# State attention and a Mish feed-forward on one core: a new order of every engine's instructions, contiguous halves of the first input, and a shorter last sum

## The chip, the cores and the metric

The kernel runs on one core of a Trainium2 chip. The metric is the device time of one execution in microseconds; the profile is of one execution, and its span runs from the first instruction to the last.

## The reference

For each of 8 batches and 8 heads, x (512 rows of 64) and a state (32 rows of 64) attend to each other in both directions. Both results go, heads side by side, as rows of 512 into a feed-forward layer of width 2048 with the Mish function.

```python
B, H, S, Ns, D = (8, 8, 512, 32, 64)          # n_tokens 4608 = 8 * (512 + 32), d_model 512, d_ff 2048
scores = scale * np.matmul(x, state.transpose(0, 1, 3, 2))
a = softmax(scores)
xread = np.matmul(a, state)
scores2 = scale * np.matmul(state, x.transpose(0, 1, 3, 2))
a2 = softmax(scores2)
sread = np.matmul(a2, x)
attn = np.concatenate([xread, sread], axis=2)  # then (B * S, H * D)
h = attn @ w_in
g = h * np.tanh(log1p(exp(h)))                 # Mish
return g @ w_out
```

## The kernel before

Since xread = a @ state, the product xread @ w_in is computed as a @ (state @ w_in): for each batch the kernel forms sw = state @ w_in (128 rows, one for each head and state row, by 2048), and multiplies the turned probabilities with it. The feed-forward width is cut into 8 slots of 256 columns.

Each large product is three matmuls of fp32r operands, 128x128 against 128x256: high by high, high by low and low by high parts. ACT writes a rounded copy (the high part) and DVE subtracts it from the original (the low part).

Batches 0 and 1 run while the weights still arrive and are split ("wide": `p`, `ma`/`mb`, `gh`, `gl`, `g`, `o` in the order strings). From batch 2 (`FIRST`) on, the work is in units of half a batch, two units for a batch, and at the end one unit of all batches' state rows. A unit has 8 periods, one for each slot, and the steps of period n are:

- `P_n` (gemm1): 12 matmuls into one of two PSUM banks (`ps_h`), 24 in the last unit. `M_n` (mish, ACT) reads that bank, so the bank is free for the next but one `P`.
- `S_n` (sums, DVE, 3 instructions), `H_n` (high, ACT), `L_n` (low, DVE): they make the seven operands of the second product, which is done with seven block products in place of eight (Strassen's scheme).
- `U_n` and `V_n` (gemm2): 12 and 9 matmuls that accumulate into four PSUM banks over the 8 periods; `U` is banks 0 and 1, `V` banks 2 and 3.
- `C` (combine): at the end of a unit one copy and 8 additions turn the four banks into the output, which is stored.

Beside this the next batch's attention runs, with letters a, b, c for a batch and the next ones:

- `SC`: 32 small matmuls (64x32 weights) give the scores; `sc tu to le x1 ts no ba ph pl` are its softmax, turns and split on ACT and DVE.
- `t2 x2 s2 TU BU RE ro`: the other direction; `TU` and `BU` go through DRAM, `RE` is 64 small matmuls (128x32 weights).
- `SX_0` and `SX_4`, each two calls of `SW` (32 small matmuls each): sw for slots 0 to 3 and 4 to 7. `xh` and `xl` split them on ACT and DVE. `SX_j` takes slots j and j+1 through the two `ps_h` banks and slots j+2 and j+3 through the two misc banks.
- `in_e` (stream): SP loads slot e of w_in (512 KB) back from `w_dram`. Slots 0 and 4 share the buffer wi6, 1 and 5 share wi7; 2, 3 and 6, 7 share the two halves of the buffer `x`. So `in_4` must wait until `SX_0` has read slot 0. `LX`, `LN` and `LS` load x, its other layout and the state, in the same buffers.

The order on each engine is written out by hand. `InOrder` ties every instruction of TensorE, DVE, ACT and SP to the one before it on that engine, so PE, for example, runs exactly in the order of the text. Batches 0 and 1 and unit 0 follow the string `OPENING`; every later period n follows the loop, which issues gemm1(n+2), high(n+1), low(n+1), mish(n+2), U(n), V(n), sums(n+2), with the other steps put in by tables (`STEADY`, `LAST`, `END`) keyed by the period.

In the opening PE also runs `fill` and `warm_up` matmuls (identity by identity), which compute nothing that is used.

The last output (state rows) is 8 transfers, four for each half of the tile `o`, all issued by SP.

Of the kernel before, what the change touches and what calls it, by code (L numbers as in the profile page):

```python
# [63 lines left out]
def state_attention_mish_kernel(ctx, tc, xT, xn, st, wiw, wow, out):  # L64
# [705 lines left out]
    run(OPENING, a=0, b=1, c=2, d=3)  # L770

    for n, (u, s) in enumerate(periods):
        if n < SLOTS:
            continue
        b, h = u
        now = SLOTS * h + s
        table = END if b == "s" else LAST if b == B - 1 else STEADY
        extra = {k: [v] for k, v in table.get(now, {}).items()}

        def beside(place):  # L780
            who = {} if b == "s" else dict(a=b, b=b + 1, c=b + 2)
            for text in extra.get(place, ()):
                run(text, **who)

        one, two = n + 1 < len(periods), n + 2 < len(periods)
        if two:
            gemm1(n + 2)
        beside("a0")
        if one:
            high(n + 1)  # L790
        beside("v0")
        if one:
            low(n + 1)
        beside("a1")
        if two:
            mish(n + 2)
        gemm2(n, 0)
        beside("pe")
        gemm2(n, 1)
        beside("pe2")  # L800
        beside("v1")
        if two:
            sums(n + 2)
        beside("a2")
        if s == SLOTS - 1:
            combine(u)
        beside("v2")
# [3 lines left out]
    lb tab lx_0 sca_0 sma_0 sma_1 lx_1 li_0 fill_1 tur_0 sca_1 top_0 sma_2 li_1 sma_3 li_2 lev_0 tur_1 Lo_0  # L811
    top_1 ev_0 tot_0 gua_0 rec_0 ci_0 hi_0 lev_1 ev_1 hi_1 warm nor_0 bac_0 ji_0 a.SW_0 pih_0 tot_1 gua_1 pil_0
    rec_1 a.wh_0 a.wl_0 hi_2 nor_1 di_2 pq_0 Lo_1 bac_1 ci_1 ji_1 ho_0 a.SW_1 js_0 li_5 li_3 pih_1 co_0 pil_1
    fill_2 fill_2 ji_2 a.wh_1 mh_0 a.wl_1 jo_0 pq_1 mh_1 a.SW_2 ho_1 a.wh_2 wo_0 gi_1 ci_5 lo_0 gj_1 gi_0 a.wl_2
    p_1 hi_3 ci_3 gj_0 ma_1 do_1 mb_1 ji_3 gh_1 g_3 g_2 jo_1 Lo_6 g_1 g_0 gl_1 a.SW_3 a.wh_3 a.wl_3 p_2 b.LX
    Lo_2 ma_2 mb_2 wo_1 lo_1 Lo_4 ho_2 p_3 hi_5 Lo_3 co_3 li_4 hi_4 g_10 do_2 gh_2 jo_2 g_13 g_12 wo_2 lo_2 gl_2
    ci_4 ji_4 ho_4 g_11 ho_3 jo_3 wo_3 ji_5 g_20 Lo_5 ho_5 li_6 g_23 a.SW_4 a.wh_4 co_5 a.wl_4 lo_3 mb_3 g_22
    g_21 ma_3 a.SW_5 p_4 js_2 co_4 gh_3 gl_3 jo_4 b.LS hi_6 ci_6 a.t2 a.wh_5 ma_4 mb_4 gh_4 a.wl_5 g_32 li_7
    wo_4 g_30 g_33 ji_6 p_5 Lo_7 gl_4 lo_4 a.x2_1 a.SW_6 a.wh_6 a.wl_6 js_5 g_31 g_41 g_42 a.x2_0 jo_5 co_6 ho_6
    g_43 ma_5 mb_5 ci_7 a.TU wo_5 lo_5 js_3 a.s2 g_40 js_6 hi_7 b.SC p_6 b.sc_1 gh_5 gl_5 b.sc_0 ji_7 g_53  # L820
    a.SW_7 mb_6 ma_6 jo_6 wo_6 b.tu b.to a.wh_7 a.wl_7 gh_6 g_50 b.le g_51 ho_7 b.x1 lo_6 b.SW_0 gl_6 p_7 js_4
    g_52 g_61 ma_7 b.wh_0 mb_7 b.ts b.no js_1 b.ba g_60 co_7 a.BU b.ph_0 a.LN b.ph_1 b.wl_0 g_62 g_63 b.pl_0
    a.RE b.LN b.pl_1 p_8 gh_7 gl_7 a.ro js_7 jo_7 wo_7 ma_8 mb_8 b.SW_2 p_9 lo_7 g_70 g_71 g_72 b.wh_2 b.wl_2
    gh_8 gl_8 mb_9 g_73 o_0 ma_9 p_10 gh_9 gl_9 mb_10 b.t2 o_1 b.SW_6 ma_10 b.wh_6 p_11 g_83 g_93 gh_10 b.wl_6
    o_2 o_3 g_81 g_91 b.SW_4 gl_10 b.x2_1 g_80 b.x2_0 c.LX ma_11 b.TU qs_0 b.wh_4 b.wl_4 g_101 qs_1 c.LS c.SC
    g_82 kh_0 kl_0 mb_11 qh_0 gh_11 gl_11 g_92 p_12 c.sc_0 ql_0 d.LS g_90 in_1 c.sc_1 in_0 c.SW_0 mb_12 qs_6
    g_102 c.wh_0 c.tu g_103 c.to kh_1 ma_12 g_113 g_100 c.le g_110 c.x1 g_112 g_111 in_5 c.t2 gh_12 gl_12 c.x2_0
    b.s2 c.wl_0 qh_1 c.ts p_13 g_121 ql_1 ma_13 c.no kl_1 mb_13 gh_13 qs_7 g_122 c.x2_1 qh_7 p_14 b.BU b.RE in_4
    gl_13 g_123 qh_6 c.ba in_2 ql_6 c.ph_0 ql_7 c.pl_0 g_133 ma_14 g_131 g_132 g_120 mb_14 b.ro qs_4 qh_4 ql_4
    in_3 c.SW_2 gh_14 g_130 c.wh_2 gl_14 c.wl_2 p_15 g_140 qs_5 ma_15 P_0 qh_5 c.SW_4 g_141 qs_3 g_142 ql_5  # L830
    mb_15 gh_15 kh_3 gl_15 qh_3 g_150 g_143 c.TU M_0 g_151 S_0 in_6 c.wh_4 in_7 kl_3 H_0 o_4 ql_3 P_1 o_5 g_152
    g_153 c.wl_4 M_1 L_0 S_1 o_6 c.ph_1 H_1 L_1 o_7 P_2 U_0 V_0 P_3 M_2 d.LX kh_7 S_2 qs_2 V_1 P_4 H_2 kh_2 kl_2
    qh_2 L_2 kh_4 kl_4 ql_2 kl_7 M_3 c.pl_1 M_4 U_1 S_3 c.SW_6 c.BU c.wh_6 kh_5 c.wl_6 c.s2 U_2 P_5 H_3 V_2 L_3
    c.LN S_4 M_5 kl_5 S_5 H_4 L_4 d.SC P_6 V_3 V_4 kh_6 kl_6 U_3 in_0 d.sc_0 M_6 S_6 d.sc_1 c.RE H_5 U_4 d.tu
    c.ro H_6 d.to P_7 L_5 U_5 L_6 V_5 M_7 S_7 H_7 d.le P_8 M_8 L_7 V_6 U_6 S_8 H_8 d.t2 L_8 P_9 in_2 U_7 M_9 S_9
    V_7 in_3 C_0 in_1
# [3 lines left out]
STEADY = {  # L840
    2: dict(pe="a.RE", pe2="b.SC", v1="a.ro", a2="b.sc_0 b.sc_1", v2="in_0 in_1 in_2 in_3"),
    3: dict(v0="b.tu"),
    4: dict(v0="b.to"),
    5: dict(v0="b.le"),
    6: dict(v0="b.t2"),
    8: dict(a2="b.x1 b.x2_0 b.x2_1"),
    9: dict(v0="b.ts b.s2", v2="b.no"),
    10: dict(v2="b.ba"),
    11: dict(pe="b.SX_0", a2="b.xh_0", v2="b.xl_0 in_4 in_5 in_6 in_7"),
    12: dict(a2="b.ph_0 b.ph_1", v2="b.pl_0 b.pl_1"),  # L850
    13: dict(v2="b.TU b.BU"),
    14: dict(pe="b.SX_4", a2="b.xh_4", v2="b.xl_4 b.LN c.LX c.LS"),
}
LAST = {
    0: dict(v2="in_0 in_1"),
    2: dict(pe="a.RE", v1="a.ro", v2="in_2 in_3"),
    7: dict(pe="ST", a2="sh", v2="sl"),
    12: dict(a2="WH_0", v2="WL_0 in_4"),
    13: dict(a2="WH_1", v2="WL_1 in_5"),
    14: dict(a2="WH_2", v2="WL_2"),  # L860
    15: dict(a2="WH_3", v2="WL_3 in_6 in_7"),
}
END = {
    0: dict(a2="WH_4", v2="WL_4"),
    1: dict(a2="WH_5", v2="WL_5"),
    2: dict(a2="WH_6", v2="WL_6"),
    3: dict(a2="WH_7", v2="WL_7"),
}
# [28 lines left out]
```

## Time and profile before

| | us |
|---|---|
| median of 3 runs (lowest to highest) | 634.57 (631.49 to 635.59) |
| the profiled execution | 632.25 |
| its span | 630.5 |
| PE busy in the span | 609.2 |
| DVE busy | 478.3 |
| ACT busy | 339.3 |

The profiled execution is 1.75 us longer than its span. The granted TensorE clock has a mean of 0.994 over the span. Busy times of different engines overlap and don't add up; for PE a busy stretch may still run at different rates, so the distance from one matmul's start to the next is read beside it.

### The profile page before, as it was taken

The numbers are of one execution on the slowest core, as the hardware profiler recorded it, in microseconds if no ns is written. First come the engines' busy times: TensorE is split into PE (matmuls) and PEld (weight loads), VectorE is DVE, ScalarE is ACT, GpSimd is POOL, SyncE is SP. The second block draws the span as 40 slices with busy tenths as digits, with TensorE's granted clock in tenths as the row PEclk, the third lists the DMA queues.
The fourth block names the chain that finished last, engine by engine and source line by source line (L and its number), as shares of the span: only waits on it lengthen the run. The fifth ranks groups of instructions, "written<-read, shape, count | busy, mean of one in ns | idle before, by whom it ended". The sixth has DMA issues, their size and how long they took to land.

```text
span 630.5 us, 15205 instructions
## 1 busy us (share of the span) xinstructions
PE 609.2 (97%) x6548; PEld 582.9 (92%) x6548; DVE 478.3 (76%) x874; ACT 339.3 (54%) x497; POOL 0.7 (0%) x6
## 2 busy tenths in 40 slices
PE   4899999899999999999999999999999999999995
PEld 3798899899999999999999999999999999999995
DVE  4786896589788888588868797679858886577753
ACT  4988763456355564347634754456534663445541
POOL 0000000000000000000000000000000000000000
PEclk9899999999999999999999999999999999999998
DMA  8976443642175234601563047403551165101201
GB/s 334 411 306 269 126 150 111 171 165 68 20 217 199 68 131 145 200 40 45 158 210 134 35 137 233 142 35 114 164 191 45 40 169 202 61 35 68 102 1 33
DMA packets 57267, 86.43 MB, mean 137 GB/s; under 512 B 35825, under 2 KB 38897, under 8 KB 54001
## 3 DMA queue, kind: packets, MB, share of 16 engines
q1 hardware_dynamic: 57056, 85.34, 40.2%
q8 instruction: 51, 0.84, 0.5%
q14 instruction: 16, 0.12, 0.1%
q10 hardware_dynamic: 144, 0.13, 0.1%
...
## 4 chain that ended last, share of the span: by engine, by line
PE 90%; ACT 4%; DVE 2%; DMA 2%; issue 1%; SPq 1%; DVEq 0%; ACTq 0%
...
## 5 line engine op out<-in xcount | busy, mean ns | idle before, releaser
L56 ACT CAST Sh<-G 128x896 fp32r<-128x896 f32 x104 | 98.2, 944 | 134.7 <-DVE G L56 48.7
L56 PE MATMUL ph_u<-aT,sw 128*128 128x256 f32 x1152 | 150.2, 280 | 0.0
L56 DVE TENSOR_TENSOR Sl<-G,Sh 128x896 fp32r<-128x896 f32 x104 | 112.9, 1086 | 44.7 <-ACT Sh L56 44.2
L56 PEld LDWEIGHTS ph_u<-aT,sw 128*128 128x128 f32 x1152 | 141.0, 189 | 2.1 <-issue 2.1
L56 DVE TENSOR_TENSOR G<-G 128x128 f32<-128x128 f32 (+1 forms) x312 | 104.7, 335 | 22.0 <-ACT G L56 14.2
L56 PE MATMUL acc<-wo,gh 128*128 128x256 f32 x512 | 90.1, 280 | 0.0
L56 ACT ACTIVATE G<-ph_u 128x512 f32<-128x512 f32 x104 | 62.2, 599 | 49.3 <-PE ph_u L56 45.9
L56 PEld LDWEIGHTS acc<-wo,gh 128*128 128x128 f32 x512 | 77.4, 188 | 3.4 <-issue 3.3
L56 PE MATMUL acc<-wo,gl 128*128 128x256 f32 x256 | 71.1, 278 | 0.0
L56 PEld LDWEIGHTS ph<-aT,sw 128*128 128x128 f32 x384 | 47.0, 193 | 8.4 <-ACT turned L56 5.0
L56 PE MATMUL ph<-aT,sw 128*128 128x256 f32 x384 | 50.3, 287 | 4.0 <-ACT turned L56 2.5
L56 ACT CAST sw<-swp 128x512 fp32r<-128x512 f32 (+1 forms) x72 | 34.3, 549 | 29.4 <-PE swp L56 29.4
L56 PEld LDWEIGHTS acc<-wo,gl 128*128 128x128 f32 x256 | 48.4, 189 | 0.0
L56 DVE TENSOR_TENSOR sw<-swp,sw 128x512 fp32r<-128x512 f32 (+1 forms) x72 | 41.0, 623 | 9.5 <-ACT sw L56 9.5
...
L56 PE MATMUL swp<-wi,bd 64*32 64x256 f32 x1024 | 33.8, 381 | 0.6 <-DVE wi L56 0.5
L56 ACT ACTIVATE turned<-ph 128x512 f32<-128x512 f32 (+1 forms) x34 | 18.5, 574 | 20.8 <-PE ph L56 16.1
L56 DVE STREAM_TRANSPOSE e<-sc 128x512 f32<-128x512 f32 x30 | 19.5, 688 | 9.5 <-ACT sc L56 9.3
...
L56 DVE CAST gh<-turned 128x1024 fp32r<-128x1024 f32 (+1 forms) x17 | 11.2, 660 | 16.3 <-ACT turned L56 9.2
L56 PE MATMUL ph_u<-srT,whl 128*128 128x256 f32 x192 | 23.1, 276 | 0.0
L56 PEld LDWEIGHTS ph_u<-srT,whl 128*128 128x128 f32 x192 | 22.4, 188 | 0.0
...
## 6 DMA issues: line engine op xcount, KB each, us to landing
...
out_dram<-o SPq DMA_DIRECT2D x32, 256.0 KB, 3.2
...
```

The lines of the kernel that those rows point to most:

```text
L56: made = method(*args, **kwargs)
```

## The change

The parts, and what each does:

- Batch 0's x comes as two arrays of halves, `x0T[h]`, contiguous in DRAM (4 KB for each partition), where before each half was cut out of a larger row in pieces of 512 bytes. Half 1 is loaded first.
- `fill` and `warm_up` multiply a zero tile, and there are more of them; `nudge` is one more small matmul of zeros.
- `sw_four` runs the two slots of the misc banks first, those of the `ps_h` banks second, in the product and in both splits.
- The block product b22 goes from bank 2 to bank 3, beside q4. So the last two additions of `combine` (256 wide, from two banks) become one of 512.
- The state rows are stored by 2 transfers in place of 8, one issued by SP and one by ACT.
- `OPENING` is rewritten. The loop and its tables are replaced by two strings, `STEADY` (run once for each of batches 2 to 6) and `CLOSING` (batch 7 and the state rows). In `STEADY` a unit's `V` comes ahead of its `U` at the start, and the small blocks `SX_0`, `SX_4`, `SC` and `RE` stand at other places.

```diff
     def load_x0(h):
-        sp.dma_start(t, xT[0][:, :, :, cols(h)])
+        sp.dma_start(t, x0T[h])
...
         def fill(self, n, pt):
             for _ in range(n):
-                pe.matmul(pt[:, :P], ident, ident, start=True, stop=True)
+                pe.matmul(pt[:, :P], zero, zero, start=True, stop=True)
...
     PRODUCTS = [(0, 0, 0, "b11"), (0, 1, 2, "b21"), (1, 0, 5, "q6"), (1, 1, 3, "q7"), (2, 0, 4, "q5"),
-                (2, 1, 6, "b22"), (3, 0, 1, "q4")]
+                (3, 0, 6, "b22"), (3, 1, 1, "q4")]
...
-        dve.tensor_add(c12, c12, m3)
-        dve.tensor_add(c21, c21, m4)
+        inner = o.rearrange("p r e -> p (r e)")[:, HALF:3 * HALF]
+        dve.tensor_add(inner, inner, acc(u, 3))
...
-                for b4 in range(4):
-                    r0 = (4 * (1 - r) + b4) * T + S
-                    sp.dma_start(out[r0:r0 + NS, :], o[cols(b4, NS), r])
+                to = out.rearrange("(b t) e -> b t e", t=T)[4 * (1 - r):4 * (2 - r), S:]
+                (act if r else sp).dma_start(to, o[:, r])
...
-        for i, bank in ((j, first_bank), (j + 2, misc)):
+        for i, bank in ((j + 2, misc), (j, first_bank)):
             sw_step(b, i, what, 2, bank)
...
+    def nudge(i):
+        pt = misc(f"nudge_{i}")
+        pe.matmul(pt[:NS, :D], zero[:D, :NS], zero[:D, :D], start=True, stop=True)
...
+    run(OPENING, 0, "abcd")
+    for b in range(FIRST, B - 1):
+        run(STEADY, b, "abc")
+    run(CLOSING, B - 1, "a")
...
 OPENING = """
+    lb tab lx_1 fill_1 fill_1 fill_1 fill_1 fill_1 fill_1 fill_1 fill_1 fill_1 fill_1 sca_1 sma_2 sma_3 lx_0
+    sca_0 sma_0 sma_1 tur_1 tur_0 top_1 fill_1 fill_1 fill_1 top_0 a.t2 les_1 li_0 lev_0 nudge_0 ci_0 warm ex_1
+    fill_1 fill_2 tot_1 gua_1 hi_0 ji_0 li_1 rec_1 a.SW_0 hi_1 nor_1 ev_0 bac_1 tot_0 ci_1 li_2 gua_0 hi_2 Lo_0
+    ji_1 fill_2 fill_2 a.wh_0 pih_1 fill_2 fill_2 rec_0 nor_0 bac_0 Lo_1 ho_0 pil_1 a.wl_0 b.LS fill_2 pih_0
+    fill_2 a.SW_1 pil_0 pq_1 co_0 a.wh_1 fill_2 ho_1 mh_1 li_5 di_2 pq_0 mh_0 gk_1 a.wl_1 b.LX gk_0 ji_2 ci_5
...
+STEADY = """
+    H_9 P_10 c.LS L_9 V_8 P_11 U_8 V_9 M_10 S_10 b.x1 b.x2_0 b.ts H_10 L_10 P_12 b.x2_1 M_11 S_11 U_9 U_10 M_12
+    S_12 H_11 L_11 V_10 b.no H_12 P_14 L_12 P_13 M_13 V_11 U_11 S_13 M_14 U_12 b.SX_0 V_12 H_13 b.xh_0 S_14 b.ba
+    b.ph_0 b.ph_1 L_13 U_13 in_4 b.xl_0 in_6 P_15 H_14 b.pl_0 M_15 in_7 in_5 L_14 P_16 S_15 b.TU M_16 b.SX_4
+    U_14 c.LX V_13 V_14 b.xh_4 b.xl_4 P_17 b.pl_1 P_18 H_15 L_15 V_15 S_16 U_15 M_17 H_16 P_20 S_17 L_16 C_1
+    M_18 S_18 V_16 U_16 H_17 b.LN L_17 P_19 V_17 H_18 L_18 M_20 U_17 b.BU M_19 S_19 H_19 P_21 V_18 U_18 c.SC
+    L_19 V_19 c.sc_1 c.sc_0 S_20 in_0 H_20 b.RE in_3 c.tu M_21 in_2 c.t2 L_20 P_23 P_22 S_21 U_19 M_22 S_22 U_20
+    V_20 H_21 L_21 V_21 U_21 c.to M_23 b.s2 S_23 H_22 L_22 H_23 L_23 P_24 M_24 S_24 V_22 c.le U_22 b.ro P_25
+    H_24 in_1 L_24 M_25 S_25 V_23 U_23 C_2
...
-    2: dict(pe="a.RE", pe2="b.SC", v1="a.ro", a2="b.sc_0 b.sc_1", v2="in_0 in_1 in_2 in_3"),
...
-    11: dict(pe="b.SX_0", a2="b.xh_0", v2="b.xl_0 in_4 in_5 in_6 in_7"),
...
-    14: dict(pe="b.SX_4", a2="b.xh_4", v2="b.xl_4 b.LN c.LX c.LS"),
...
+CLOSING = """
+    P_10 H_9 L_9 M_10 U_8 ST V_8 S_10 sh sl P_11 H_10 L_10 M_11 U_9 V_9 S_11 P_12 H_11 L_11 M_12 U_10 V_10 S_12
...
+    H_21 L_21 M_22 U_20 V_20 S_22 P_23 H_22 L_22 M_23 U_21 V_21 S_23 H_23 L_23 U_22 V_22 U_23 V_23 C_2
```

## Rows read from the trace of the kernel before

**Rows 1.** The page: busy us, share of the span and instructions, by engine.

```profile
PE 609.2 (97%) x6548; PEld 582.9 (92%) x6548; DVE 478.3 (76%) x874; ACT 339.3 (54%) x497; POOL 0.7 (0%) x6
```

**Rows 2.** Busy time by stretches of 10 us: length, engines (instructions), PEclk, DMA, GB/s.

```profile
10.00:20.00 10.00, 6.89 (x64) 5.40 (x63) 8.77 (x18) 9.29 (x13) 0.00 (x0) 0.83 1.00 399
20.00:30.00 10.00, 7.88 (x76) 7.14 (x77) 8.65 (x14) 8.83 (x14) 0.00 (x0) 1.00 1.01 428
...
60.00:70.00 10.00, 9.06 (x84) 7.97 (x83) 8.98 (x14) 7.51 (x12) 0.00 (x0) 1.00 0.00 0
...
120.00:130.00 10.00, 8.24 (x96) 7.59 (x95) 6.44 (x13) 3.04 (x7) 0.00 (x0) 1.00 0.65 169
```

**Rows 3.** Waits of PE: who waited for whom, us, times, longest.

```profile
PE ph L56 <- ACT turned L56: 2.5, 3, 2.1
...
PE sc L56 <- DMA bd<-in_st_dram: 1.8, 1, 1.8
```

**Rows 4.** The chain that ended last: start, us, what (and how many).

```profile
26.58 1.17 ACT wor L56
...
123.86 1.10 PE sc L56 x32
...
127.88 2.72 PE ph L56 x24
...
297.13 1.93 PE swp L56 x64
300.30 1.36 PE ph_u L56 x12
...
310.50 1.89 PE swp L56 x64
...
313.64 1.41 PE ph_u L56 x12
...
330.38 1.02 PE sc L56 x32
...
335.49 1.41 PE ph_u L56 x12
...
533.29 1.03 PE srp L56 x64
535.54 1.36 PE ph_u L56 x12
```

**Rows 5.** Tile wi, 228 to 240.5: PE's matmuls of SX_0, the loads after it.

```profile
L56 PE MATMUL swp<-wi,bd x64: 376/376/400, 228.7 to 230.3; 64*32 64x256 f32 x64
L56 SPq DMA_DIRECT2D wi<-w_dram x4: 320/336/731, 229.5 to 231.2; - x4
...
DMA to landing us min/median/max: 4.2/5.1/6.2
```

**Rows 6.** The loads of tile wi in 433 to 447 (a later batch).

```profile
L56 SPq DMA_DIRECT2D wi<-w_dram x4: 319/326/426, 434.6 to 436.3; - x4
...
DMA to landing us min/median/max: 3.2/6.7/7.9
```

**Rows 7.** DVE groups of one batch, 262.9 to 331.3: count, busy us, mean ns.

```profile
L56 DVE TENSOR_TENSOR sw<-swp,sw 128x512 fp32r<-128x512 f32 x8 | 5.0, 684 | 1.6 <-ACT sw L56 1.6
```

**Rows 8.** Timeline of the end: start, us, instructions, count.

```profile
623.54 1.08 DVE L56 TENSOR_TENSOR o_s<-o_s,acc_('s', 0)_2_7795 128x256 f32<-128x256 f32 x3
624.54 0.41 DVE L56 TENSOR_TENSOR o_s<-o_s,acc_('s', 0)_3_7802 128x256 f32<-128x256 f32 x1
624.65 3.64 SPq L56 DMA_DIRECT2D out_dram<-o_s  x8
```

**Rows 9.** DMA issues of the last output: KB each, us to landing.

```profile
out_dram<-o_s SPq DMA_DIRECT2D x8, 64.0 KB, 1.7
```

**Rows 10.** DMA issues in 102 to 112.5 us: batch 0's first two stores.

```profile
out_dram<-o SPq DMA_DIRECT2D x2, 256.0 KB, 2.3
```

**Rows 11.** First input: busy time in 3 to 5 us, columns as before.

```profile
3.00:5.00 2.00, 0.00 (x0) 0.00 (x0) 0.00 (x0) 0.00 (x0) 0.00 (x0) 1.00 1.10 328
```

More of the change, by code (lines that the diff above doesn't have):

```diff
@@ L25 @@
 HALF = S // 2
-WARM = 5
+WARM = 14
 FIRST = 2
@@ L63, in state_attention_mish_kernel @@
 @with_exitstack
-def state_attention_mish_kernel(ctx, tc, xT, xn, st, wiw, wow, out):
+def state_attention_mish_kernel(ctx, tc, x0T, xT, xn, st, wiw, wow, out):
     nc = tc.nc
@@ L90, in state_attention_mish_kernel @@
     make_identity(nc, ident)
+    zero = pool.tile([P, P], F32, name="zero")
+    nc.vector.memset(zero, 0.0)
     w_dram = dram.tile([SLOTS, P, NC * 2 * P], F32, name="w_dram")
@@ L107, in load_xT @@
             for i in range(2):
-                sp.dma_start(xTs[b][i], xT[b][:, i])
+                sp.dma_start(xTs[b][i], xT[b - 1][:, i])
             return
@@ L111, in load_xT @@
         xTs[b] = [t[:, i] for i in range(2)]
-        sp.dma_start(t, xT[b])
+        sp.dma_start(t, xT[b - 1])
     def load_xn(b, tag="x"):
@@ L491, in stream @@
         else:
-            if e % 2 == 0:
-                streams["x"] = pool.tile([P, 2, NC, 2 * P], F32, tag="x", name=f"wi_{e}")
-            t = streams["x"][:, e % 2]
+            x = streams.pop(e ^ 1, None)
+            if x is None:
+                x = streams[e] = pool.tile([P, 2, NC, 2 * P], F32, tag="x", name=f"wi_{e}")
+            t = x[:, e % 2]
         w_in[e] = t
@@ L631, in combine @@
     def combine(u):
-        (m1, m2), (m6, m7), (m5, m3), (m4, _) = ((a[:, :HALF], a[:, HALF:]) for a in (acc(u, t) for t in range(4)))
+        (m1, m2), (m6, m7), (m5, _) = ((a[:, :HALF], a[:, HALF:]) for a in (acc(u, t) for t in range(3)))
         o = pool.tile([P, 2, DM], F32, tag="o", name=f"o_{u[0]}_{u[1]}")
@@ L694, in warm_up @@
         for _ in range(WARM):
-            pe.matmul(warm[:, :P], ident, ident, start=True, stop=True)
+            pe.matmul(warm[:, :P], zero, zero, start=True, stop=True)
     pw = {}
@@ L740, in state_attention_mish_kernel @@
         "o": lambda i: out_wide(*divmod(i, 4)),
-        "fill": lambda n: a0.fill(n, acc(0, 3)), "qs": q_sums, "qh": q_high, "ql": q_low, "kh": q7_high, "kl": q7_low, "in": stream,
+        "nudge": lambda i: nudge(i), "fill": lambda n: a0.fill(n, acc(0, 3)), "qs": q_sums, "qh": q_high, "ql": q_low, "kh": q7_high, "kl": q7_low, "in": stream,
         "WH": ws_high, "WL": ws_low,
@@ L750, in state_attention_mish_kernel, with run @@
     }
-    def run(text, **batch):
+    def run(text, first, letters):
+        batch = {who: first + i for i, who in enumerate(letters)}
+        n0 = 2 * SLOTS * max(0, first - FIRST)
         for step in text.split():
@@ L763, in run @@
             elif what in ("U", "V"):
-                gemm2(i, what == "V")
+                gemm2(n0 + i, what == "V")
             elif what == "C":
-                combine(units[i])
+                combine(units[n0 // SLOTS + i])
+            elif what in "PMSHL":
+                common[what](n0 + i)
             else:
                 common[what](i)
[L770 to L807, printed above, removed]
@@ L810 @@
-OPENING = """
[L811 to L836, printed above, removed]
@@ L837 @@
-"""
-STEADY = {
-    2: dict(pe="a.RE", pe2="b.SC", v1="a.ro", a2="b.sc_0 b.sc_1", v2="in_0 in_1 in_2 in_3"),
[L842 to L848, printed above, removed]
-    11: dict(pe="b.SX_0", a2="b.xh_0", v2="b.xl_0 in_4 in_5 in_6 in_7"),
-    12: dict(a2="b.ph_0 b.ph_1", v2="b.pl_0 b.pl_1"),
-    13: dict(v2="b.TU b.BU"),
-    14: dict(pe="b.SX_4", a2="b.xh_4", v2="b.xl_4 b.LN c.LX c.LS"),
-}
@@ L854 @@
[L854 to L868, printed above, removed]
+    run(OPENING, 0, "abcd")
+    for b in range(FIRST, B - 1):
+        run(STEADY, b, "abc")
@@ new lines @@
+"""
+CLOSING = """
+    P_10 H_9 L_9 M_10 U_8 ST V_8 S_10 sh sl P_11 H_10 L_10 M_11 U_9 V_9 S_11 P_12 H_11 L_11 M_12 U_10 V_10 S_12
+    P_13 H_12 L_12 M_13 U_11 V_11 S_13 P_14 H_13 L_13 M_14 U_12 V_12 S_14 WH_0 WL_0 in_4 P_15 H_14 L_14 M_15
+    U_13 V_13 S_15 WH_1 WL_1 in_5 P_16 H_15 L_15 M_16 U_14 V_14 S_16 WH_2 WL_2 P_17 H_16 L_16 M_17 U_15 V_15
+    S_17 WH_3 C_1 WL_3 in_6 in_7 P_18 H_17 L_17 M_18 U_16 V_16 S_18 WH_4 WL_4 P_19 H_18 L_18 M_19 U_17 V_17 S_19
+    WH_5 WL_5 P_20 H_19 L_19 M_20 U_18 V_18 S_20 WH_6 WL_6 P_21 H_20 L_20 M_21 U_19 V_19 S_21 WH_7 WL_7 P_22
+    H_21 L_21 M_22 U_20 V_20 S_22 P_23 H_22 L_22 M_23 U_21 V_21 S_23 H_23 L_23 U_22 V_22 U_23 V_23 C_2
@@ L871 @@
+"""
 def kernel(**inputs):
@@ L879 @@
     turned = state.reshape(B, NC, 2, NS, D).transpose(0, 4, 2, 1, 3).reshape(B, D, 2, NC * NS)
+    xT = x6.transpose(0, 5, 6, 2, 1, 4, 3).reshape(B, P, 2, NC, HALF)
     arrays = {
-        "in_xT_dram": x6.transpose(0, 5, 6, 2, 1, 4, 3).reshape(B, P, 2, NC, HALF),
+        "in_x0T_dram": xT[0].reshape(P, 2, NC, 2, P).transpose(3, 0, 1, 2, 4),
+        "in_xT_dram": xT[1:],
         "in_xn_dram": x.reshape(B, NC, 2, P, NT, D).transpose(0, 3, 1, 2, 4, 5),
```

22 lines of the change are left out of this document (added).

## Prediction

> **What bounds the kernel now.** I read the page's engine line first: PE is busy for 609.2 of 630.5 us [rows 1], so 21 us at most is to be had from idle time of PE. The table by stretches says where: 10 to 20 lacks 3.11 us, 20 to 30 lacks 2.12, 60 to 70 lacks 0.94 and 120 to 130 lacks 1.76 [rows 2]; nearly all the rest is the first 10 us and the tail. The table of waits names two of them: `ph` waits for ACT's `turned` (Mish), and the scores of a later batch for the state's load [rows 3].
>
> A busy PE still has two speeds, and the chain of waits shows them. Twelve `ph_u` matmuls take 1.36 us in some stretches and 1.41 in others, of the same instruction and both at the full granted clock: 0.05/12 = 4.2 ns each. The speed changes at the blocks of small matmuls. After `SX_0` (297.13) it is 1.36, after `SX_4` (310.50) 1.41, and so until the next `RE` and `SC`; after the `SC` at 330.38 it is 1.41, and where the last `RE` (533.29) has no `SC` behind it, it is 1.36 and stays so to the end [rows 4]. I read this as a toggle: each block of 32 or 64 small matmuls turns one speed into the other. One block doesn't fit: the `SC` at 123.86, which came out of a wait of 1.8 us, was followed by the fast speed (2.72 for 24) though the fast speed stood ahead of it. So a wait can undo a toggle.
>
> **The tail.** Of 8 issues by SP, 3.64 us in all, the last ends at 624.65 + 3.64 = 628.29; a transfer lands 1.7 us after the start of its issue, the last at 629.6 [rows 8, 9]. The last addition ends at 624.54 + 0.41 = 624.95. After: the two last additions, which start 0.33 us apart and take 0.41, become one of 512 columns for 0.68 us (the nearest row of a DVE instruction of that width that reads PSUM [rows 7]), so the sum ends at about 624.9 as before. Both transfers are then issued at once on two queues; a store of 256 KB lands 2.3 us after its issue [rows 10], and I add 0.3 us as two run together: 627.5. That is 629.6 - 627.5 = **-2.0 us** (estimate, from -2.4 if they don't disturb each other to -1.2 if one waits for the other). b22's move to bank 3 changes no count of matmuls: nothing.
>
> **The opening.** Order, fills and the half loads go together, as they decide one thing, when PE runs without idling. Three items have rows. The wait for the state's load goes, since `LS` now stands well ahead of `SC`: -1.76. The stall at 60 to 70 I count as gone: -0.94 [rows 2]. Against it, ACT now does `ho_1` (1.17 us [rows 4], at 26.58) ahead of `mh_1`, on which the second half of `pq` waits as it does now: +1.17. The sum is **-1.5 us**. Ends: -4.8 if the 2.12 us of 20 to 30 go too and `ho_1` is hidden; +2.4 if the two stalls come back elsewhere and `ho_1` and the moved `t2` (an estimate of the same size) both lie on the path, because ACT and DVE are busy for 9.29 and 8.77 of 10 us there. The fills (zero by zero) stand in stretches where PE waits, so I count them at nothing; what hides them is that wait, and a fill that overruns costs about its own length.
>
> Batch 0's x moves at 328 GB/s in 3 to 5 us against 399 and 428 later [rows 2, 11]; at the later rate its 0.5 MB would be there some 0.4 us sooner. I leave that within the ends. The Trainium skill (DMA: Bandwidth & Descriptors, Specifications) gives at least 512 bytes as the smallest transfer at line rate; the old pieces are 512 bytes, so by that rule contiguous halves gain nothing. The row, with 328 of 428, doesn't agree fully.
>
> **The batches.** I walked the queues of PE, ACT and DVE through `STEADY` by hand (a period is 12 + 12 + 9 matmuls on PE). By that walk `L_n` is ready ahead of `U_n` and `V_n` everywhere, with the least margin, about half a microsecond, at `V_17` and at `U_16` after `C_1`. One place doesn't hold, and it is the DMA queue's.
>
> `SX_4` reads slots 4 to 7. Their loads can start only when `SX_0` has read slot 0, and SP issues `in_4` first, so `in_6`, `in_7` and `in_5` queue behind it. Before, slot 0 was read first in `SX_0`, and `in_4` was issued 229.5 - 228.7 = 0.8 us after its start. After, the misc half goes first, and slot 0 comes half a block (1.93/2 = 0.96 us) later: 1.75 us after the start of `SX_0`, which I call T. From the first issue to the last landing the four loads take 231.2 + 6.2 - 229.5 = 7.9 us in the first of five stretches, 436.3 + 7.9 - 434.6 = 9.6 in the longest; the median of the five is 8.4 [rows 5, 6]. So slot 5 is there at T + 10.15. Before, `SX_4` started at T + 13.4 (310.50 - 297.13 [rows 4]) and nothing waited. Now PE has between the two blocks only `V_12`, `U_13`, `P_15` and `P_16`, 45 matmuls: 45 x 0.113 = 5.1 us (5.3 at the slow speed). `SX_4` starts at T + 1.93 + 5.1 = T + 7.0, and needs slot 5 three quarters through, at T + 8.45. It waits 10.15 - 8.45 = 1.7 us, 1.5 at the slow speed; I take 1.6. With 7.9 us and the slow speed it is 0.95, with 9.6 us and the fast one 2.9. `STEADY` runs five times: 5 x 1.6 = **+8.0 us** (4.8 to 14.5). What queues behind it on PE is the whole rest of the batch; nothing gives the time back, since PE had no idle time there to absorb it.
>
> **The two speeds.** Counting matmuls between the blocks, before: 288 slow ones from `SC` to `SX_0`, 99 fast, 132 slow from `SX_4` to `RE`, 9 fast. That is 420 of 528 in each of four batches and 366 in the first, none after the last `RE`: 2046 slow. After, in the order of `STEADY`: `RE` 300 `SX_0` 45 `SX_4` 174 `SC` 9 `RE`. In the last run `SC` is left out, and 744 matmuls follow the last `RE`. If `RE` is followed by the fast speed, 4 x (45 + 9) + 45 + 744 = 1005 are slow, 1041 fewer: 1041 x 4.2 ns = -4.4 us. If it is followed by the slow one, 4 x (300 + 174) + 300 + 183 = 2379, 333 more: +1.4 us. The wait inside `SX_4` may undo its toggle, and then the batches alternate. I take the middle, **-1.5 us**, and keep both ends.
>
> The Trainium skill (TensorEngine Tiling (Array Packing), Key Properties) says only that a change of the tiling mode drains TensorE. The number of blocks stays, so by that rule alone the new places of the blocks are worth 0; it has nothing on the speed after a block, which the chain shows.
>
> **Sum.** -2.0 - 1.5 + 8.0 - 1.5 = +3.0 us. On the profiled execution's own 632.25 us that is 635.25. The median of the runs is 2.32 us above it, so I forecast 637.6 us, 0.5% more: no change by what can be told here, which is about 1%, or 628.2 to 640.9 us.
>
> **Rivals.**
> - The loads don't hold `SX_4` up and the speeds fall well: -2.0 - 1.5 - 4.4 + 0.5 = -7.4, 627.2 us. For it: a first load lands 3.2 us after its issue at best [rows 6], and 0.52 MB at 428 GB/s is 1.2 us [rows 2], so four could be there in 3.2 + 3 x 1.2 = 6.8, with hardly a wait (0.1 x 5 = 0.5). Against it: the shortest of five is 7.9 us.
> - The wait at its upper end, on the other side: transfers of 9.6 us in every batch make it 2.9 x 5 = 14.5, so -2.0 - 1.5 + 14.5 - 1.5 = +9.5, 644.1 us. It decides from the loads' time: each microsecond over 8.4 costs 5, and 9.1 us brings the sum to +6.3, the bound of slower. For it: one batch of five showed it.
> - The slow speed after `RE` throughout: +1.4 in place of -1.5, 640.5 us. It is settled by the parity of blocks and waits in the opening. From `b.SC` on the opening has 14 blocks, an even number, so with no wait the speed ahead of them comes back behind them; before, the wait at 123 turned it.
> - The opening does not fill its idle time, as ACT and DVE, not PE, set it: +2.4 in place of -1.5, 641.5 us.
>
> **Chances.** Forecast 0.47 (its own range 633 to 642; slower by over 1% in 0.06 of it), no wait 0.22 (faster by over 1% in 0.16 of it), the long wait 0.12, the slow speed 0.11 (slower in 0.04), the opening 0.08 (slower in 0.05). Faster by over 1%: 0.16 and 0.01 for what I don't see, 0.17; slower: 0.06 + 0.12 + 0.04 + 0.05 and 0.01, 0.28; the rest, 0.55, is within 1%. The range runs from 628 to 645: it takes in the long wait and reaches into the no-wait case.
>
> **What would show it.** In the waits of PE, `swp` for the DMA `wi<-w_dram`, in all some 8 us and one or more a batch; `SX_4` (64 `swp`) at 3.5 us from first to last in place of 1.9. In the chain, `ph_u` x12 at 1.36 or 1.41 between `RE` and the next `SX_0`. At the end two transfers, and 2.6 us from the last addition to the last landing. In the stretches of 60 to 70 and 120 to 130, a full PE. The prediction is wrong if the loads land within 6.7 us of the first issue, or if PE waits for DVE in the batches, at `V_17` or `U_16` first.

## The result and the profile after

| | before | after |
|---|---|---|
| median of 20 runs each, us | 634.56 | 637.85 |
| lowest to highest | 631.49 to 639.15 | 633.54 to 642.22 |
| the profiled execution | 632.25 | 638.50 |
| its span | 630.46 | 636.71 |

The ratio is 1.0051, 95% interval 1.0033 to 1.0068: 0.5% more, no change by the bound of 1%. The forecast was 637.6. It came out by errors that cancelled, as the profile shows.

The page, busy us by engine, which answers to [rows 1]:

```profile
PE 615.5 (97%) x6620; PEld 584.7 (92%) x6620; DVE 477.5 (75%) x859; ACT 337.3 (53%) x497; POOL 0.7 (0%) x6
```

Stretches of the changed kernel, columns as in [rows 2]:

```profile
10.00:20.00 10.00, 9.94 (x107) 8.72 (x107) 8.83 (x17) 9.04 (x12) 0.00 (x0) 1.00 1.01 419
20.00:30.00 10.00, 7.92 (x85) 7.06 (x89) 7.99 (x13) 8.37 (x17) 0.00 (x0) 1.00 1.02 428
60.00:70.00 10.00, 10.00 (x99) 9.46 (x98) 9.21 (x15) 9.94 (x13) 0.00 (x0) 1.00 1.02 418
120.00:130.00 10.00, 9.55 (x103) 8.93 (x103) 7.92 (x16) 3.80 (x8) 0.00 (x0) 1.00 0.72 238
```

The stall at 60 to 70 is gone, the one at 20 to 30 is not. Much of the 9.94 us in 10 to 20 is fills, which compute nothing. The waits of PE, as in [rows 3]:

```profile
PE swp L56 <- DMA wi<-w_dram: 5.6, 9, 1.2
PE ph L56 <- ACT turned L56: 2.1, 1, 2.1
```

The wait for the state's load (`bd`) is gone, and the wait that the prediction had put in `SX_4` is there. The chain, as [rows 4] (start, us, what), shows one `SX_4` that the loads hold up, and the speed of PE behind three `RE`:

```profile
228.83 1.54 PE swp L56 x48
...
232.49 5.95 DMA wi<-w_dram
...
238.48 0.67 PE swp L56 x16
...
272.50 1.41 PE ph_u L56 x12
...
345.52 1.36 PE ph_u L56 x12
...
546.20 1.41 PE ph_u L56 x12
```

The chain leaves `SX_0` for a load that its reading releases, and comes back to PE for the last quarter of `SX_4`. Tile wi in the same stretch and in the one with the longest loads answers to [rows 5, 6]; first 228 to 242:

```profile
L56 SPq DMA_DIRECT2D wi<-w_dram x4: 320/381/1165, 230.4 to 232.5; - x4
...
DMA to landing us min/median/max: 3.8/4.6/6.0
```

and 365 to 380:

```profile
L56 SPq DMA_DIRECT2D wi<-w_dram x4: 327/380/424, 368.5 to 369.9; - x4
...
DMA to landing us min/median/max: 3.5/5.6/7.8
```

`in_4` goes out 1.6 us after the start of `SX_0`, and the last load lands 8.1 us (232.5 + 6.0 - 230.4) and 9.2 us (369.9 + 7.8 - 368.5) behind it. By the starts of its matmuls each of the five `SX_4` takes 2.94 to 4.04 us from its first matmul to the next block's first, where before it took 1.89 [rows 4]: 7.4 us in all.

The end, as [rows 8] (start, us, instruction, count), and one stretch of its transfers, columns as in [rows 2]:

```profile
626.56 0.69 DVE L56 TENSOR_TENSOR o_s<-o_s,acc_('s', 0)_3_7825 128x512 f32<-128x512 f32 x1
627.27 0.69 SPq L56 DMA_DIRECT2D out_dram<-o_s  x1
627.28 1.40 ACTq L56 DMA_DIRECT2D out_dram<-o_s  x1
```

```profile
632.00:633.00 1.00, 0.00 (x0) 0.00 (x0) 0.00 (x0) 0.00 (x0) 0.00 (x0) 0.50 0.26 102
```

From the end of the last addition (627.25) to the end of the span, which is called the tail here, are 9.5 us; before they were 630.46 - 624.95 = 5.5. The two stores move 102 GB/s with 0.26 of the DMA engines' time.

The span grew by 6.25 us. With the distance of every matmul to the next put to its cause, that is: tail +4.0, `SX_4` +7.2 (its 7.4 less 0.2 lost in blocks of before), speeds -2.5, opening -2.9, other gaps +0.4. The medians differ by 3.3 only: the profile of before is of a short execution, 2.3 us under its median, and that of after lies 0.65 over its own. Experiments e10 and e11 show where the profile of before is short.

### The profile page after: what moved, and what is told of

It reads as the page before. It is cut to its first block, busy times and chain, and to the rows that moved or that the text cites. A ratio compares the mean times of both kernels' runs of the same rounds, so it can differ in the third digit from the quotient of the medians.

```text
span 636.7 us, 15344 instructions
## 1 busy us (share of the span) xinstructions
PE 615.5 (97%) x6620; PEld 584.7 (92%) x6620; DVE 477.5 (75%) x859; ACT 337.3 (53%) x497; POOL 0.7 (0%) x6
## 4 chain that ended last, share of the span: by engine, by line
PE 86%; DMA 10%; ACT 1%; SPq 1%; DVE 0%; issue 0%; DVEq 0%
PE ph_u L56 22%; PE acc L56 13%; PE ph L56 7%; DMA wi<-w_dram 7%; PE swp L56 4%; DMA wor<-in_wo_dram 2%; PE srp L56 1%; PE sc L56 1%; SPq L56 1%; PE acc_('s', 0)_0_7807 L56 1%; PE acc_(2, 0)_0_2392 L56 1%; PE acc_(7, 1)_0_7378 L56 1%; PE acc_(7, 1)_1_7385 L56 1%; PE acc_(3, 0)_0_3304 L56 1%; PE acc_(7, 1)_3_7406 L56 1%; PE acc_(3, 0)_1_3311 L56 1%
## 5 line engine op out<-in xcount | busy, mean ns | idle before, releaser
L56 PE MATMUL ph_u<-aT,sw 128*128 128x256 f32 x1152 | 145.0, 278 | 0.0
L56 PEld LDWEIGHTS ph_u<-aT,sw 128*128 128x128 f32 x1152 | 137.7, 188 | 0.9 <-issue 0.4
L56 ACT ACTIVATE G<-ph_u 128x512 f32<-128x512 f32 x104 | 60.6, 598 | 84.1 <-PE ph_u L56 64.5
L56 PEld LDWEIGHTS ph<-aT,sw 128*128 128x128 f32 x384 | 45.6, 188 | 5.7 <-ACT turned L56 3.1
L56 PE MATMUL ph<-aT,sw 128*128 128x256 f32 x384 | 48.2, 281 | 2.1 <-ACT turned L56 2.1
L56 PE MATMUL swp<-wi,bd 64*32 64x256 f32 x1024 | 36.2, 383 | 6.0 <-DMA wi<-w_dram 5.6
L56 PEld LDWEIGHTS swp<-wi,bd 64*32 64x32 f32 x1024 | 15.8, 105 | 17.3 <-DMA wi<-w_dram 10.7
L56 DVE TENSOR_TENSOR gl<-turned,gh 128x1024 fp32r<-128x1024 f32 (+1 forms) x17 | 19.7, 1159 | 2.5 <-ACT gh L56 1.9
```

The lines of the kernel that those rows point to most:

```text
L56: made = method(*args, **kwargs)
```

## The experiments

Ratios are to the kernel before, with 95% intervals; "base" names the kernel that was edited.

**e1_old_stores** (base: after) puts the eight stores back.

```diff
-                (act if r else sp).dma_start(to, o[:, r])
+                for b4 in range(4):
+                    sp.dma_start(out[r0:r0 + NS, :], o[cols(b4, NS), r])
```

> The changed kernel with the 8 stores of before, by SP. Theory (the two stores are the slow part of the tail: the profile after shows 9.4 us from the last addition to the end of the span, 5.5 before): 4.0 us less than the changed kernel, about 633.9 us, ratio to before 0.999, and again about 5.5 us from the last addition to the end, at a DMA share of about 0.5 in place of 0.26. Rival (my prediction's term: two stores save 2.0 us, and the long end is the waiting of the program for something else): 2 us more than the changed kernel, about 639.9 us, ratio 1.008.

635.26 us, ratio 1.0008 (0.9976 to 1.0040). Its end and one stretch of its transfers:

```profile
624.43 0.69 DVE L56 TENSOR_TENSOR o_s<-o_s,acc_('s', 0)_3_7825 128x512 f32<-128x512 f32 x1
625.14 3.63 SPq L56 DMA_DIRECT2D out_dram<-o_s  x8
```

```profile
627.00:628.00 1.00, 0.00 (x0) 0.00 (x0) 0.00 (x0) 0.00 (x0) 0.00 (x0) 0.50 0.53 146
```

The tail is 5.8 us again (631.0 - 625.12), 3.7 less than after. By the ratios the run is 2.7 us faster than after, where 4.0 was expected; its interval takes in both. Eight issues one after the other move 146 GB/s, two big ones 102.

**e2_two_stores** (base: before) does that part alone, the other way round: the two stores in the old kernel.

> The kernel before with only the last output's two stores (SP and ACT) in place of eight. Theory (two stores are slow): 4.0 us more than before, about 638.6 us, ratio 1.006, DMA share 0.26 at the end. Rival (prediction): 2.0 us less, 632.6 us, ratio 0.997.

638.88 us, ratio 1.0064 (1.0036 to 1.0093), 4.1 us slower. The same share of the DMA engines stands at its end:

```profile
629.07 0.41 DVE L56 TENSOR_TENSOR o_s<-o_s,acc_('s', 0)_3_7802 128x256 f32<-128x256 f32 x1
629.18 0.69 SPq L56 DMA_DIRECT2D out_dram<-o_s  x1
629.51 1.16 ACTq L56 DMA_DIRECT2D out_dram<-o_s  x1
```

```profile
634.00:635.00 1.00, 0.00 (x0) 0.00 (x0) 0.00 (x0) 0.00 (x0) 0.00 (x0) 0.50 0.26 102
```

The tail is 9.2 us. So the store alone makes the tail 3.7 us longer, with the other parts (9.5 against 5.8) or without them (9.2 against 5.5).

**e9_pair_stores** (base: after) asks what sets the 0.26: four stores of two batches each in place of two of four. By the dimension, the share halves; by the size or the number of issues, it would not fall.

```diff
+                for k in range(2):
+                    b0 = 4 * (1 - r) + 2 * k
+                    to = out.rearrange("(b t) e -> b t e", t=T)[b0:b0 + 2, S:]
+                    (act if r else sp).dma_start(to, o[cols(k, 2 * NS), r])
```

> The changed kernel with four stores of two batches each (64 rows) in place of two of four batches. Theory (a store's outermost dimension, the batches, is what is spread over the DMA engines, so four batches keep 4 of 16 busy, the DMA share 0.26 that the end showed): two batches keep 2 busy, the share at the end is 0.13 and the tail about 5 us longer than 9.4, ratio to before 1.013. Rival 1 (large stores are slow by their size): the tail is shorter than 9.4, about 7.5, ratio 1.002. Rival 2 (each store has engines of its own): four stores of two on 8 engines, tail about 7, ratio 1.001.

644.5 us, ratio 1.0129 (1.0082 to 1.0176). The profiled execution is longer than that, 650.3; only its end is read here:

```profile
633.09 0.69 DVE L56 TENSOR_TENSOR o_s<-o_s,acc_('s', 0)_3_7825 128x512 f32<-128x512 f32 x1
633.81 1.25 SPq L56 DMA_DIRECT2D out_dram<-o_s  x2
```

```profile
644.00:645.00 1.00, 0.00 (x0) 0.00 (x0) 0.00 (x0) 0.00 (x0) 0.00 (x0) 0.50 0.13 51
```

The share is 0.13 and the tail 14.7 us (648.5 - 633.8), 5.2 more than after; the median of the other three runs, 643.1, is 5.2 us above that of after. 0.26 is about 4 of 16 engines and 0.13 about 2: the share goes with the slowest dimension of the store, the batches, and not with the number or the size of the stores. The Trainium skill (DMA: Bandwidth & Descriptors, Rules for kernel authors) has this rule: an outermost dimension of fewer than 16 confines a transfer to at most so many engines. The traces agree, 0.26 beside 4/16 and 0.13 beside 2/16.

**e3_sx4_later** (base: after) moves `SX_4` and what needs it behind `U_14` and `V_13`, some 2.4 us. `H_15`, `L_15` and `V_15` come sooner, so that PE has work behind `SX_4`.

```diff
-    ... P_16 S_15 b.TU M_16 b.SX_4 U_14 c.LX V_13 V_14 b.xh_4 b.xl_4 P_17 b.pl_1 P_18 H_15 L_15 V_15 S_16 ...
+    ... P_16 S_15 b.TU M_16 U_14 H_15 L_15 V_13 b.SX_4 V_14 c.LX b.xh_4 V_15 b.xl_4 P_17 b.pl_1 P_18 S_16 ...
```

> The changed kernel with SX_4 moved behind U_14 and V_13 in STEADY (H_15, L_15 and V_15 drawn ahead, so that PE has V_14 and V_15 between SX_4 and P_17). SX_4 then starts some 9.4 us after SX_0 in place of 7.0. Theory (SX_4 waits for the loads that follow SX_0): the waits of swp for wi fall from 5.6 us to under 1.5, SX_4 takes 1.9 to 2.2 us in every batch in place of 2.9 to 4.0, 7 us less than the changed kernel, about 630.8 us, ratio to before 0.994. Rival (the time only moves: P_17 then waits for the banks that ACT and DVE split, or the loads are late by as much again): about 637.9 us, ratio 1.005.

631.25 us, ratio 0.9952 (0.9917 to 0.9986), 6.3 us less than after by the ratios. Its waits of PE have only this left of it:

```profile
PE swp L56 <- DMA wi<-w_dram: 0.2, 1, 0.2
```

All five `SX_4` take 1.89 us again. The wait is a cost of the place, not of the block. The profile is 8.5 us shorter than that of after: 7.4 are the wait, and 1.2 are 276 fewer slow matmuls behind the opening (4.45 ns each).

**e8_old_slot_order** (base: after) reads the slots and loads them in the old order, so that `in_4` goes out sooner.

```diff
-        for i, bank in ((j + 2, misc), (j, first_bank)):
+        for i, bank in ((j, first_bank), (j + 2, misc)):
...
-    ... in_4 b.xl_0 in_6 P_15 H_14 b.pl_0 M_15 in_7 in_5 L_14 ...
+    ... in_4 b.xl_0 in_5 P_15 H_14 b.pl_0 M_15 in_6 in_7 L_14 ...
```

> The changed kernel with the slots of SX in the old order (the ps_h banks' first) and the loads in the order 4, 5, 6, 7. The first load can then start 0.8 us after the start of SX_0 in place of 1.75. Theory (SX_4 waits for the last of four loads, whose clock starts when slot 0 is read): the wait falls from 1.5 to about 0.7 us a batch, not to nothing, so SX_4 takes 2.3 to 3 us, 3.7 us less in all than the changed kernel, ratio to before 0.999. Rival (the wait comes from the order of the banks or from the loads' own rate alone): 1.005 as the changed kernel.

637.54 us, ratio 1.0041 (1.0017 to 1.0066): nearly nothing of it shows in the runs. The loads did go out earlier, 0.8 us after the start of `SX_0`, and the weight loads of PE waited 2.1 us for them in place of 10.7. But they had a new wait:

```profile
PEld swp L56 <- ACT G L56: 3.1, 5, 0.6
...
PEld swp L56 <- DMA wi<-w_dram: 2.1, 4, 0.7
```

With the old order `SX_4` begins with the `ps_h` bank that `P_16` has just filled, so it waits 0.6 us for `M_16`, five times of five. `SX_4` still loses 4.7 us in place of 7.4. The profile is 2.1 us shorter than that of after: 2.7 less in `SX_4`, and 1.2 more because 276 more matmuls of the batches and the end ran at the slow speed (x 4.45 ns). By the ratios the gain is 0.6 us, give or take some 2; so the runs neither show the 2.7 nor rule them out.

**e4_old_opening** (base: after) puts the old `OPENING` back (with `WARM` 5).

> The changed kernel with the OPENING string (and the 5 warm-up matmuls) of before; contiguous halves and all else stay. Theory (the new opening saves what its idle time says, 2.9 us between the two profiles): 2.9 us more than the changed kernel, about 640.7 us, ratio to before 1.010, give or take up to 4 us for the matmul speed that the batches inherit. Rival (the opening's idle time is set by ACT, DVE and DMA, the new order only fills it with matmuls of zeros): no more than 0.5 us from the changed kernel, 637.9 us, ratio 1.005.

645.36 us, ratio 1.0151 (1.0108 to 1.0194), 6.3 us more than after, more than twice the 2.9 of the theory. In its profile the opening ends 6.6 us later (217.8 against 211.1 us, the end of the last matmul of batch 2's first half). The first of its waits of PE:

```profile
PE sc L56 <- DMA bd<-in_st_dram: 7.3, 2, 5.0
```

5.0 of the 7.3 us is the first wait of all, for the first inputs, which the profile of before puts down to `xT` (5.2 us). The other 2.3 us is the `SC` whose wait in the profile of before is 1.8 [rows 3]; the granted clock falls there to 0.50 from 126 to 128 us.

**e11_state_sooner** (base: before) undoes that wait alone.

```diff
-    ... b.x2_0 c.LX ma_11 b.TU qs_0 b.wh_4 b.wl_4 g_101 qs_1 c.LS c.SC
+    ... b.x2_0 c.LS c.LX ma_11 b.TU qs_0 b.wh_4 b.wl_4 g_101 qs_1 c.SC
```

> The kernel before with one move: the load of batch 2's state (c.LS) stands ahead of c.LX and b.TU on SP in the opening, where it stood just ahead of c.SC. Theory (the scores' wait for it, 1.8 to 2.6 us, is the largest item of the old opening, and it also undid a turn of the rate): the wait goes, -2.2 us, and every block behind it turns the other way, so 1305 slow matmuls follow the opening in place of 2046, -3.3 us, +0.4 in the opening itself: 5.1 us less, ratio 0.992. Rival 1 (the wait is worth its own length only): 0.9965. Rival 2 (something else is late next): 1.000.

630.57 us, ratio 0.9922 (0.9900 to 0.9944). No wait for `bd` is left in its trace. That is 5.0 us by the ratio and 4.2 by the medians, for a wait of 1.76 us by the profile of before. The size is the expected one, but the trace doesn't show the expected way to it. PE comes to this `SC` at 124.2 us, later than in the profile of before, and the opening ends at 214.7, 0.5 later than there. From the last blocks of the opening on the speeds are those of the profile of before, until an `SX_0` at 366 us turns nothing; most stretches behind it run at the other speed, with some 620 slow matmuls fewer in all, 2.8 us. So the two profiles alone don't show what the wait is worth. What the wait does in an execution like this one is seen in the next run.

**e10_blocks_before** (base: before) puts two whole blocks of 32 small matmuls, which compute nothing, behind `C_0 in_1` and behind the last `RE`.

```diff
+    def block(i):
+        ...
+                    pe.matmul(pts[u][o, cols(k, HALF)], ident[half(u), o], srds[half(u), 0:2].rearrange("p b k d -> p (b k d)"), ...
-    V_7 in_3 C_0 in_1
+    V_7 in_3 C_0 in_1 block_0
-    2: dict(pe="a.RE", v1="a.ro", v2="in_2 in_3"),
+    2: dict(pe="a.RE", pe2="block_1", v1="a.ro", v2="in_2 in_3"),
```

> The kernel before with two whole blocks of 32 small matmuls (64x32 weights, 256 columns, as SC, results unused) at the places where the single small matmuls stood: behind the opening and behind the last RE. The single ones left the rate as it was. Theory (a block of 32 or more turns the rate, a short one doesn't): the batches show ph_u x12 at 1.36 where before shows 1.41 and the other way round, the stretch behind the last RE stays fast, some 640 slow matmuls in place of 2046, 6.2 us less, and the two blocks cost 2.0: 4.1 us less, ratio 0.9935. Rival (the rate belongs to the place in the batch): 2.0 us more, ratio 1.003.

636.13 us, ratio 1.0014 (0.9998 to 1.0031): no gain. The first block in the chain:

```profile
217.52 0.68 PE acc_(2, 0)_2_2283 L56 x6
...
218.54 1.02 PE block L56 x32
...
221.18 0.71 PE acc_(2, 1)_0_2774 L56 x6
```

Behind the second, at 540.0, the matmuls are 113.4 ns apart from start to start, ahead of it 117.3. Both blocks turned the speed. The gain did not follow, since the stretch ahead of the first was fast already in this execution, where in the profile of before it is slow; the two had parted in the opening, which is the same code in both. Stretches of e10 at the wait for `bd`, columns as in [rows 2]:

```profile
124.00:126.00 2.00, 0.19 (x2) 0.00 (x0) 1.32 (x4) 0.00 (x0) 0.00 (x0) 1.00 0.93 173
126.00:128.00 2.00, 1.32 (x32) 0.79 (x32) 0.00 (x0) 0.00 (x0) 0.00 (x0) 0.74 0.13 34
128.00:130.00 2.00, 2.00 (x18) 1.61 (x8) 0.00 (x0) 0.00 (x0) 0.00 (x0) 0.50 0.29 61
130.00:132.00 2.00, 2.00 (x18) 2.00 (x17) 0.86 (x2) 1.37 (x4) 0.00 (x0) 0.91 1.01 254
```

and the same place before:

```profile
122.00:124.00 2.00, 0.24 (x9) 0.17 (x16) 1.24 (x4) 0.00 (x0) 0.00 (x0) 1.00 0.75 169
124.00:126.00 2.00, 2.00 (x41) 1.52 (x34) 0.00 (x0) 0.00 (x0) 0.00 (x0) 1.00 0.04 8
```

Here PE waits 2.5 us, and then the granted clock falls to 0.50, the level of 1.2 GHz: 2 x (0.26 + 0.50 + 0.09) = 1.7 us lost. Together 4.2 us. PE comes to this wait at 124.0 us, as it comes to the same `SC` at 124.2 in e11, which has no wait; e11's opening ends 3.8 us sooner (214.7 against 218.5). The profiles of e2 and e5, which have the same opening, show 2.6 and 2.5 us and the same fall to 0.50. So the profile of before, with 1.76 us and a clock of 1.00, was the mildest of four. The end of its opening shows the same:

```profile
213.90 0.35 PE acc_(2, 0)_3_2290 L56 x3
```

It ends at 214.3 us, where e10 has 218.5, e2 218.8 and e5 (next) 216.5 with the same code.

**e5_nudged_before** (base: before) tries single small matmuls at the same two places.

```diff
-    V_7 in_3 C_0 in_1
+    V_7 in_3 C_0 in_1 nudge_0
-    2: dict(pe="a.RE", v1="a.ro", v2="in_2 in_3"),
+    2: dict(pe="a.RE nudge_1", v1="a.ro", v2="in_2 in_3"),
```

> The kernel before with two single small matmuls (64x32 weights, nothing uses them) added: one at the end of the opening, one behind the last RE. Theory (a block of small matmuls turns PE's rate for the large ones from 113.3 to 117.8 ns a matmul or back, and nothing else sets it): each flips the rate of all that follows, so behind the opening some 640 slow matmuls remain in place of 2046, 6.2 us less, about 628.4 us, ratio 0.990; the batches show ph_u x12 at 1.36 from SC to SX_0 and from SX_4 to RE, 1.41 from SX_0 to SX_4. Where a wait in the opening has already turned the rate in a run, that run is as before or slower, so the median may gain less. Rival (the rate belongs to the place in the batch, or a single matmul on one tile doesn't turn it): ratio 1.000.

635.24 us, ratio 1.0004 (0.9984 to 1.0024). The chain around the first:

```profile
215.39 0.71 PE acc_(2, 0)_2_2283 L56 x6
...
216.45 0.23 PE nudge L56 x2
...
218.28 0.71 PE acc_(2, 1)_0_2758 L56 x6
```

This single small matmul turned nothing, nor did the one behind the last `RE` (113.3 ns ahead of it, 113.4 behind). The theory held for blocks, not for this.

**e6_later_8_stores** (base: e3) puts the eight stores back, four on each queue.

```diff
+                for b4 in range(4):
+                    r0 = (4 * (1 - r) + b4) * T + S
+                    (act if r else sp).dma_start(out[r0:r0 + NS, :], o[cols(b4, NS), r])
```

> The changed kernel with SX_4 moved as in the run before and the last output in 8 stores of 32 rows, four issued by SP and four by ACT. Theory (waits for the loads and slow stores are the two losses, and they add): from the last addition to the end 4.0 us (three issues of 0.45, the landing and 0.9 to the end) in place of 9.4, so 5.4 us less than the run with SX_4 moved alone, ratio to before 0.987. Rival (two queues gain nothing over one, as the transfers run at what the engines give): 5.5 us from the last addition to the end, ratio 0.989; if the tail is no loss on the median, 0.995.

626.84 us, ratio 0.9877 (0.9835 to 0.9919). Two stretches of its transfers:

```profile
620.00:621.00 1.00, 0.00 (x0) 0.00 (x0) 0.00 (x0) 0.00 (x0) 0.00 (x0) 1.00 0.66 160
621.00:622.00 1.00, 0.00 (x0) 0.00 (x0) 0.00 (x0) 0.00 (x0) 0.00 (x0) 1.00 0.99 277
```

Two queues with 32 rows outermost fill the DMA engines (0.99) and the tail is 4.5 us, a microsecond less than before and 4.9 less than in e3. By the ratios the run is 4.8 us faster than e3, of 5.4 expected.

**e7_later_nudged** (base: e6) has one small matmul ahead of `CLOSING`, and **e12_best_block** (base: e6) a whole block there.

```diff
-    P_10 H_9 L_9 M_10 U_8 ST V_8 ...
+    nudge_1 P_10 H_9 L_9 M_10 U_8 ST V_8 ...
```

```diff
-    P_10 H_9 L_9 M_10 U_8 ST V_8 ...
+    block_1 P_10 H_9 L_9 M_10 U_8 ST V_8 ...
```

> As the run with SX_4 moved and 8 stores on two queues, and one small matmul at the start of CLOSING. Theory (the rate is a toggle): the last 600 matmuls run at 113.3 ns in place of 117.8, 2.7 us less, ratio to before 0.983. Rival: 0.987, as without it.

> The changed kernel with SX_4 moved and 8 stores on two queues (the fastest so far, ratio 0.988), with one whole block of 32 unused small matmuls at the start of CLOSING. Theory (such a block turns the rate): the last 600 matmuls at 113.3 in place of 117.8 ns, 2.7 us less, the block costs 1.0: 1.65 us less, ratio 0.985, in a profile whose CLOSING is slow ahead of it. Rival: 1.0 us more, 0.989.

626.21 us (0.9867, 0.9829 to 0.9904) and 625.64 us (0.9845, 0.9814 to 0.9877): neither can be told from e6. In the profile of e7 the end was fast on both sides of the nudge; its batches had 855 slow matmuls where those of e6, in the same order, had 413. Both begin at the same speed. In e7 it changes in the middle of a stretch of large matmuls, with no block there:

```profile
447.37 1.36 PE ph_u L56 x12
...
451.25 1.41 PE ph_u L56 x12
```

Between the two, one matmul starts 192 ns after the last; e6 has a step of 186 ns at that place and stays fast. In the profile of e12 (633.3 us, longer than its median) the block turned the fast speed into the slow one:

```profile
551.91 0.68 PE acc_(7, 0)_1_7001 L56 x6
552.59 1.02 PE block L56 x32
...
555.22 0.71 PE acc_(7, 1)_0_7396 L56 x6
```

That makes three blocks of three that turned the speed and three single matmuls of three that did not. Which speed the last stretch begins with differed between e6 and these two, so a block put in by hand gains in one execution and loses in another. That e12 has the lowest median shows nothing of the block.

## Why the prediction was right, point by point

**The number was right by cancellation.** The sum was +3.0 on the profiled execution and the median 2.32 above that. Measured were +6.25 on the profile, and a median 0.65 below it. The tail was 6.0 us worse than predicted; the other four terms came out 1.4, 0.6, 1.0 and 3.0 better, 6.0 together. That is luck. Each term:

| term | predicted, us | measured, us |
|---|---|---|
| tail | -2.0 | +4.0 |
| opening | -1.5 | -2.9 |
| wait in `SX_4` | +8.0 | +7.4 |
| two speeds | -1.5 | -2.5 |
| median over the profiled execution | +2.3 | -0.65 |

**The tail is the step that failed.** Its first half held: the one addition of 512 columns took 0.69 us (684 ns in [rows 7]) and the issues followed at once. The failing sentence is "a store of 256 KB lands 2.3 us after its issue [rows 10]". That row is of a tile whose slowest dimension is its 128 rows; the new store's is 4 batches. After its issue the span goes on for 9.4 us (636.71 - 627.27), and e1, e2 and e9 show that this shape alone does it: with 4 outermost a share of 0.26, with 2 a share of 0.13, with 32 rows on two queues 0.99. The bounds of the term, -2.4 to -1.2, left no room for it. The row was near in size and far in shape, and the shape decides. (The subtraction 629.6 - 627.5 gives -2.1, not -2.0, which changes nothing.)

**The wait in `SX_4` held**, with its place and size: 1.6 us was forecast for each batch, and 1.05, 1.14, 2.15, 1.96 and 1.06 us were lost. `in_4` was issued 1.6 us after the start of `SX_0` (1.75 forecast), `SX_4` began 7.4 us after it (7.0). e3 takes the wait away by the place alone and gains 6.3 us. That slot 0 comes half a block later is right too, but e8 shows the other side, which the prediction did not see: with the old order the block needs the `ps_h` bank of the `P` just ahead of it, and waits for Mish there.

**The opening** gave more than its sum. `ho_1` ahead of `mh_1` was charged at 1.17 us. It does lie on the chain of after, for 1.06 us ahead of Mish's table load and `turned`:

```profile
20.68 1.06 ACT wor L56
...
23.04 0.39 ACT turned L56
```

But ACT's work ahead of it begins sooner, and `turned` comes only 0.3 us later than before:

```profile
21.44 1.28 ACT L56
...
22.73 0.40 ACT turned L56
```

So the wait of `ph` for `turned` stayed at 2.1 us, the longest of [rows 3]. The sum -1.76 - 0.94 + 0.3 = -2.4 is near the -2.9 measured, but no run parts the order, the fills and the halves, so the items are not shown one by one. The sum also has no term for the clock: [rows 2] shows 0.83 in 10 to 20, at most 1.7 us lost, and after it is 1.00. The 2.12 us of 20 to 30 did not go, as the lower end had allowed.

**The price of the wait for the state's load was too low.** 1.76 us is what one execution shows. Three profiles with the same code at that place show 2.5 to 2.6 us and a fallen clock, about 4.2 us with both, and e11, which undoes this wait alone, gains 4.2 by the medians. That the two agree is in part chance, as e11's trace shows; but beside e10, which comes to that place at the same time, its opening is 3.8 us shorter. The openings say the same of the whole: that of after ends at 211.1 us, 3.1 ahead of the profile of before and 5.3 to 7.7 ahead of e5, e10 and e2. The median of before stands 2.3 us over its profile. So the 2.3 us that the prediction carried over to the median of after did not belong there: they are mostly of the old opening, which the change replaces. How much of them is not is open, since the two speeds differ between executions as well. e4 fits: the old opening costs 6.3 us by the ratios and 6.6 in the profiles.

**The two speeds**: blocks of 32 or 64 small matmuls mostly turn the speed, and a wait can undo it. In e3, where nothing holds `SX_4` up, all five turned it; in after three of the five held-up ones did. So the batches changed course as forecast, with 1422 slow matmuls in batches and end where there were 2036. The middle of the bounds was a fair choice, but no more than that: e6 and e7 run the same batches with 413 and 855. What stays open is what sets the starting speed in the opening, why a few blocks turn nothing although no wait of over 0.1 us stands ahead of them (`SX_0` at 439 in e10 and at 366 in e11), and why the speed changes without a block at 450 in e7 and at 251 in e12. So the toggle of the prediction is a good rule for most blocks, not the whole cause.

**The rivals.** "No wait" (627.2) fell with the first `swp` in the table of waits; e3 shows what it would have been worth. "The slow speed after `RE` throughout" fell: behind the last six `RE` it was 1.41 twice and 1.36 four times. "The long wait" fell: the longest was 2.2 us, and the longest stretch of loads 9.2. "The opening does not fill" fell: PE is full at 60 to 70, and e4 shows what the old opening costs.

**What is left.** The change has one gain that stands, the opening, and two losses that can be had back apart: e6 has neither and is 1.2% faster than before, 1.7% faster than after. A microsecond of that is e6's own, from its second queue.
